# Chunk attention with a cosine router: v loaded by pairs of chunks over all partitions, five tiles ahead

## The chip, the cores and the metric

The kernel runs on one core of one Trainium2 chip. The metric is the device time in microseconds; before the change it is 676.58 us, the median of 3 runs (675.12 to 679.66).

## The reference

Attention works within chunks of 64 positions: batch 8, 8 heads, 576 positions (9 chunks), head size 64, all float32. Its result goes, token by token (4608 tokens of 512), into a mixture of 8 experts with one expert per token.

```python
scores = scale * np.matmul(q_c, k_c.transpose(0, 1, 2, 4, 3))   # per chunk of 64
attn = np.exp(scores - np.max(scores, axis=-1, keepdims=True))
attn = attn / (np.sum(attn, axis=-1, keepdims=True) + 1e-09)
out = np.matmul(attn, v_c)
x = out.transpose(0, 2, 1, 3).reshape(B * S, H * D)
logits = xn @ en.T / tau                     # rows of x and of expert_emb normalised
expert_idx = np.argmax(logits, axis=1)
h = np.maximum(x[mask] @ w1[e], 0.0)         # for each expert e
out[mask] = gate_w[mask, None] * (h @ w2[e])
```

## The kernel before

The order of the work is written out by hand (`manual_schedule`): every engine and every DMA queue takes its instructions in the order in which the code emits them.

**Attention** runs over 36 tiles of 128 tokens, that is two chunks each. Since a batch has 9 chunks, a tile can hold the last chunk of one batch and the first of the next (tiles 4, 13, 22, 31). The 8 heads are 4 pairs; "parity" (`par`) is the head within its pair, even or odd. One pass of the loop at L1037 does, for several tiles at once, the steps of a software pipeline: `turn_qk(t + 3)` (L603) transposes q and k on TensorE; `scores(t + 2)` (L616) multiplies them, in 32 matmuls of 64x64 that use a quarter of the array each, and takes maximum and difference on VectorE; `weights(t + 2)` (L642) is the exponential on ScalarE; `turn_a(t)` (L646) transposes the weights; `values(t)` (L655) multiplies them by v, whose 65th column is 1 so that the row sum comes with it, and divides; `turn_x(t - 1)` (L689) transposes the result. After every four tiles come `logits`, `pick` and `place` (L702, L729, L745), which choose the experts and compute each token's place, and `put` (L810) scatters tile after tile to the DRAM tensor `spots` through GpSimd's queue.

In `scores` the array's rows are chosen by the parity and its columns by the chunk c of the tile. Even heads write one PSUM bank and odd heads another. The transposed weights `aT` therefore have even heads on partitions 0 to 63 and odd heads on 64 to 127, for both chunks, and v has to lie the same way.

**Loads.** `load_qk(t)` (L574) brings q and k of a tile, on GpSimd's queue except the first four k; it runs four tiles ahead of the transposes. `load_v(b)` (L592) brings a whole batch, one DMA a head on SyncE's queue, each onto 64 partitions; two buffers `v_sb` (L457) take turns. The first batch comes in two portions (L1009 and L1048). Batch 1 is issued at the end of step 1 (L1092), and batch b from 2 on (L1064) right after the values of the tile that reads the last chunk of batch b - 2:

```python
b = (2 * t + 2) // NCB + 1
if b not in v_t and b < B and t > 1:
    load_v(b)
```

SyncE's queue also takes, in the order of the code: nine clears of `spots` from step 1 on (L1090), `load_first` of w1 at step NT - 8 = 28 (two DMAs of 2 MB, L1067), the same for w2 at step 30 (L1069), and `load_early` (L807, at steps 26, 27, 28 and 33), which reads the first tokens of experts 0 and 7 back from `spots` and so waits for the puts emitted before it.

**Experts.** Hidden products of the first two blocks (`early_parts`, L1025, from step 34) stand between the last attention tiles. Then come 35 further blocks of 128 tokens in a row, and each reads its w1 and w2 by expert from DRAM.

Of the kernel before, what the change touches and what calls it, by code (L numbers as in the profile page):

```python
# [9 lines left out]
FP32 = mybir.dt.float32  # L10
# [8 lines left out]
P = 128  # L19
CH = 64  # L20
# [5 lines left out]
def kernel(  # L26
# [11 lines left out]
    nc = tc.nc  # L38
    B, H, S, Dh = q.shape
# [3 lines left out]
    NPAIR = H // 2  # L43
    KD = D // P
    KF = F // P
    NT = N // P
    NCB = S // CH
# [39 lines left out]
    def pad(pool, n, name):  # L87

        if n:
            nc.gpsimd.memset(pool.tile([P, n], FP32, tag=name, name=name, bufs=1), 0.0)  # L90
# [33 lines left out]
    def load_first(buf, rows):  # L124

        for s in range(2):
            e = (0, E - 1)[s]
            nc.sync.dma_start(out=whole(buf[s]), in_=rows[:, e : e + 1, :], max_dma_last_dim=4096)
# [316 lines left out]
    VW = 2 * Dh  # L445
    with (
# [7 lines left out]
    ):  # L454

        pad(one, 40, "pad_one")
        v_sb = [one.tile([P, NPAIR, NCB, VW], FP32, name=f"v{i}") for i in range(2)]  # L457
        NX = 2 * RB
        xr = one.tile([P, NX, W], FP32, name="xr")
        blank = one.tile([P, W], FP32, name="blank")  # L460
# [108 lines left out]
            nc.sync.dma_start(out=spots[SPARE : SPARE + G, :], in_=blank[0:G])  # L569

        before = one.tile([P, E], BF16, name="before")
        qk_t, qkT, v_t, st = {}, {}, {}, {}

        def load_qk(t):  # L574

            for src, nm, eng in (
                (k, "kx", nc.sync if t < 4 else nc.gpsimd),
                (q, "qx", nc.gpsimd),
            ):
                x = qk_p.tile([P, H, Dh], FP32, tag=nm, name=nm)  # L580
                done = 0
                while done < P:
                    b, s = divmod(t * P + done, S)
                    n = min(P - done, S - s)
                    eng.dma_start(  # L585
                        out=x[done : done + n],
                        in_=src[b, :, s : s + n, :].rearrange("h p d -> p h d"),
                    )
                    done += n
                qk_t[nm, t] = x.rearrange("p h d -> p (h d)")  # L590

        def load_v(b, c0=0, c1=NCB, eng=nc.sync):  # L592

            t = v_sb[b % 2]
            for h in range(H):
                r0 = CH * (h % 2)
                eng.dma_start(
                    out=t[r0 : r0 + CH, h // 2, c0:c1, 0:Dh],
                    in_=v[b, h].rearrange("(c k) d -> k c d", k=CH)[:, c0:c1],
                )  # L600
            v_t[b] = t

        def turn_qk(t):  # L603
            for nm in ("kx", "qx"):
# [11 lines left out]
        def scores(t):  # L616
            qx, kx = qkT.pop(("qx", t)), qkT.pop(("kx", t))
            ps = ps_s.tile([P, 2, 512], FP32, tag="sc", name="sc")
            sc = ps[:, :, 0 : NPAIR * CH].rearrange("p r (i k) -> p r i k", k=CH)
            for i in range(NPAIR):  # L620
                for par in range(2):
                    for c in range(2):
                        r0, c0 = CH * par, CH * c
                        nc.tensor.matmul(
                            sc[CH * c : CH * c + CH, par, i],
                            lhsT=qx[r0 : r0 + CH, i, c0 : c0 + CH],
                            rhs=kx[r0 : r0 + CH, i, c0 : c0 + CH],
                            start=True,
                            stop=True,
                        )  # L630
            mx = wk.tile([P, 2, NPAIR], FP32, tag="mx", name="mx")
            nc.vector.tensor_reduce(mx, sc, axis=AX.X, op=ALU.max)
            a = wk.tile([P, NPAIR, 2, CH], FP32, tag="a", name="a", bufs=3)
            nc.vector.tensor_tensor(
                a.rearrange("p i r k -> p r i k"),
                sc,
                mx.unsqueeze(3).to_broadcast([P, 2, NPAIR, CH]),
                ALU.subtract,
            )
            st[t] = {"a": a}  # L640

        def weights(t):  # L642
            a = st[t]["a"]
            nc.scalar.activation(a, a, AF.Exp, scale=scale)
# [10 lines left out]
        def values(t):  # L655
            d = st[t]
            ps = ps_v.tile([P, 2, 512], FP32, tag="pv", name="pv")
            pv = ps[:, :, 0 : NPAIR * (Dh + 1)].rearrange("p r (i d) -> p r i d", d=Dh + 1)
            for i in range(NPAIR):
                for par in range(2):  # L660
                    for c in range(2):
                        b, cb = divmod(2 * t + c, NCB)
                        r0 = CH * par
                        nc.tensor.matmul(
                            pv[CH * c : CH * c + CH, par, i],
                            lhsT=d["aT"][r0 : r0 + CH, i, CH * c : CH * c + CH],
                            rhs=v_t[b][r0 : r0 + CH, i, cb, 0 : Dh + 1],
                            start=True,
                            stop=True,
                        )  # L670
            rs = wk.tile([P, 2, NPAIR], FP32, tag="rs", name="rs")
            nc.vector.tensor_scalar(rs, pv[:, :, :, Dh], 1e-9, None, ALU.add)
            nc.vector.reciprocal(rs, rs)
            x = xr[:, t % NX, 0:D]
            nc.vector.tensor_tensor(
                x.rearrange("p (i r d) -> p r i d", r=2, d=Dh),
                pv[:, :, :, 0:Dh],
                rs.unsqueeze(3).to_broadcast([P, 2, NPAIR, Dh]),
                ALU.mult,
            )  # L680
            nc.gpsimd.iota(
                xr[:, t % NX, D + TOK : D + TOK + 1].bitcast(I32),
                pattern=[[0, 1]],
                base=P * t,
                channel_multiplier=1,
            )
            st[t] = {"x": x}
# [106 lines left out]
        def count_early():  # L794

            cnt = rt_ps[:, 3, 0]
            nc.tensor.matmul(cnt, lhsT=onesb, rhs=before, start=True, stop=True)

            nc.vector.tensor_scalar(full, cnt, -1.0, lim, ALU.mult, ALU.add)
            nc.vector.tensor_scalar(full, full, 0.0, float(P), ALU.max, ALU.min)  # L800
            with nc.allow_low_precision("whole numbers up to 36 + 128"):
                nc.vector.tensor_tensor(eqb_all[:, 0], full, ends_e, ALU.mult)
                nc.vector.tensor_tensor(before, before, eqb_all[:, 0], ALU.add)
# [202 lines left out]
        load_qk(1)  # L1006
        for x in v_sb:
            nc.vector.memset(x[:, :, :, Dh : Dh + 1], 1.0)
        load_v(0, 0, 4)  # L1009
        load_qk(2)  # L1010
        load_qk(3)
        norm_experts()
        nc.gpsimd.memset(xr[:, :, D:W], 0.0)
# [23 lines left out]
        for t in range(-3, NT + 3):  # L1037

            if 0 <= t < NT:
                turn_a(t)  # L1040
            if t == early_t - 1:
                count_early()
            if t + 3 < NT:
                turn_qk(t + 3)
                if t + 7 < NT:
                    load_qk(t + 7)
            if t == -2:
                load_v(0, 4, NCB)  # L1048
            if t - 2 in ends:
                logits(ends[t - 2])  # L1050
            if t == NT:
                turn_x(t - 1)
            early_parts(t, 0)
            if 0 <= t + 2 < NT:
                scores(t + 2)
            if t - 2 in ends:
                copy_logits(ends[t - 2])
            if 0 <= t - 1 < NT - 1:
                turn_x(t - 1)
            if t - 3 in ends:  # L1060
                place(ends[t - 3])
            if 0 <= t < NT:
                values(t)
                b = (2 * t + 2) // NCB + 1  # L1064
                if b not in v_t and b < B and t > 1:
                    load_v(b)
            if t == NT - 8:  # L1067
                load_first(w1_sb, w1_rows)
            if t == NT - 6:  # L1069
                load_first([w[0] for w in w2_sb], w2_rows)  # L1070
            if 0 <= t + 2 < NT:
                weights(t + 2)
            if t - 2 in ends:
                pick(ends[t - 2])
            if early_t <= t < early_t + XBUF:
                load_early(t - early_t)

            put(1 if t < NT - 2 else 2)
            if t == NT - 3:
                turn_xb(0)  # L1080
                load_early(XBUF)
            if t == NT - 1:
                turn_xb(1)
            early_parts(t, 1)
            if t == -2:
                turn_experts()
            if t >= 0:
                next(constants, None)
            if t >= 1:
                next(clears, None)  # L1090
                next(clears, None)
            if t == 1:  # L1092
                load_v(1)
        groups()
        pad_places()
        put(len(to_put))
# [23 lines left out]
    with (  # L1120
# [18 lines left out]
        for j in range(LEAST - 1):  # L1139
            n = j + 2  # L1140
# [104 lines left out]
```

## Time and profile before

| | us |
|---|---|
| median of 3 runs | 676.58 |
| profiled execution, its own time | 675.66 |
| its span, first to last instruction | 673.8 |
| first values of tile 0 start | 19.6 |
| values of tile 35 (the last) start | 164.2 |
| second expert product of block 0 starts | 189.5 |
| TensorE matmul busy | 628.7 |
| mean granted TensorE clock | 0.988 of full |

In the profile, PE is TensorE (PEld its weight loads), DVE VectorE, ACT ScalarE, POOL GpSimd; a name with q is the engine's sequencer or DMA queue, so SPq is SyncE's. A row of the timeline has start and length in us, engine, line, operation, output <- inputs, the count, and in brackets the engine's idle time before it and what ended that. A row of the windows has, after the stretch and its length, busy us and instruction count of PE, PEld, DVE, ACT and POOL, then granted clock, DMA share and GB/s. In the page's slices each digit is the busy share in tenths of one fortieth of the span.

### The profile page before, as it was taken

The page shows a single profiled execution, that of the slowest core. Times are in us where ns is not written, and L with a number is a line of the kernel's source. Part 1 is how long each engine was busy: PE and PEld are TensorE (multiplying, and loading weights), DVE is VectorE, ACT ScalarE, POOL GpSimd, SP SyncE. Part 2 cuts the span into 40 slices and gives each one's busy share as a digit, 9 for nine tenths or more (in the row PEclk, how much of TensorE's full clock was granted, in tenths as well). Part 3 has the DMA queues.
Part 4 walks back from the last instruction along what each step waited for, and adds up shares of the span by engine and source line. Part 5 has one row for each costly group of instructions (what it writes and reads, how often), then busy time and mean ns, then how long its engine had stood idle before and what let it go on. Part 6 is the DMA issues. An engine that isn't in the chain of part 4 may idle for free. (4 is left out here: it accounts for less than half of the span.)

```text
span 673.8 us, 24854 instructions
## 1 busy us (share of the span) xinstructions
PE 628.7 (93%) x9744; PEld 366.8 (54%) x9744; DVE 420.9 (62%) x1140; ACT 445.8 (66%) x776; POOL 158.4 (24%) x237
## 2 busy tenths in 40 slices
PE   5989999999789999999999999999999999999993
PEld 4867777776446667667434444334444444444441
DVE  3848888887469555656575466767654666564430
ACT  4746667666124777677877867778777777877650
POOL 6738887743311000000100100001001000100101
PEclk9979999999989999999999999999999999999998
DMA  9998899989918711112777111776821114411101
GB/s 249 235 246 235 240 293 267 266 231 348 363 54 302 279 51 46 43 40 71 293 262 282 57 37 48 281 281 228 330 70 44 44 48 162 172 43 34 51 28 37
DMA packets 94686, 112.66 MB, mean 167 GB/s; under 512 B 52460, under 2 KB 72684, under 8 KB 94552
## 3 DMA queue, kind: packets, MB, share of 16 engines
q1 hardware_dynamic: 82824, 72.84, 33.8%
q0 software_dynamic: 11696, 38.04, 17.1%
q8 instruction: 81, 1.33, 0.8%
q14 instruction: 53, 0.43, 0.2%
q10 hardware_dynamic: 32, 0.02, 0.0%
HBM read 334.71 MB, written 22.69 MB: 530 GB/s over the span
## 5 line engine op out<-in xcount | busy, mean ns | idle before, releaser
L413 PE MATMUL y_ps<-w,hT 128*32 128x512 f32 (+1 forms) x2368 | 272.6, 589 | 0.0
L361 ACT ACTIVATE h<-C 64x256 f32<-64x256 f32 x264 | 178.6, 677 | 95.5 <-DVE C L374 68.9
L413 PEld LDWEIGHTS y_ps<-w,hT 128*32 128x32 f32 x2368 | 103.3, 110 | 142.3 <-issue 110.2
L428 POOL DMA_INDIRECT out_dram<-y,spot x36 | 36.1, 1002 | 436.9 <-ACT y L421 208.8
L374 DVE TENSOR_TENSOR C<-C,h 128x256 f32<-128x256 f32 x231 | 96.1, 416 | 49.2 <-DVEq L299 42.5
L342 PE MATMUL h<-w,S 128*32 128x256 f32 x1056 | 95.6, 379 | 0.0
L342 PE MATMUL h<-sums,xbT 128*32 128x256 f32 x1056 | 94.8, 379 | 0.0
L342 PE MATMUL h<-w,xbT 128*32 128x256 f32 x1056 | 78.5, 380 | 7.1 <-ACTq L299 6.0
L368 DVE STREAM_TRANSPOSE hT<-h 128x512 f32<-128x512 f32 x66 | 46.7, 708 | 44.1 <-ACT h L361 44.0
L342 PEld LDWEIGHTS h<-w,xbT 128*32 128x32 f32 x1056 | 43.0, 110 | 39.8 <-ACTq L299 13.4
L342 PEld LDWEIGHTS h<-w,S 128*32 128x32 f32 x1056 | 50.4, 110 | 20.3 <-ACT w L301 0.4
L342 PEld LDWEIGHTS h<-sums,xbT 128*32 128x32 f32 x1056 | 50.0, 110 | 20.3 <-ACT C L377 0.6
L227 DVE TENSOR_SCALAR rn<-rn 128x1 f32<-128x1 f32 x37 | 5.7, 153 | 68.9 <-ACT rn L224 68.9
L342 PE MATMUL h<-sums,S 128*32 128x256 f32 x528 | 47.8, 379 | 0.0
L813 POOL DMA_INDIRECT spots<-xr,dest x36 | 37.4, 1039 | 30.3 <-DVE dest L778 9.0
L203 DVE STREAM_TRANSPOSE xbT<-xin 128x256 f32<-128x256 f32 x73 | 44.2, 643 | 0.5 <-DVE hT L368 0.5
L224 ACT ACT_TABLE_LOAD x34 | 43.6, 1283 | 0.9 <-issue 0.3
L231 ACT ACT_TABLE_LOAD x34 | 43.6, 1283 | 0.6
L421 ACT ACTIVATE y<-y_ps,gate 128x512 f32<-128x512 f32 (+1 forms) x37 | 25.2, 682 | 24.1 <-issue 8.8
L695 ACT COPY xT<-tr 128x512 f32<-128x512 f32 x36 | 21.1, 586 | 29.8 <-PE tr L693 25.4
L585 POOL DMA_DIRECT2D kx<-in_k_dram x36 | 32.0, 891 | 19.7 <-PE tr L608 18.8
L585 POOL DMA_DIRECT2D qx<-in_q_dram x40 | 34.5, 866 | 1.6 <-PE tr L608 0.8
(202 smaller groups left out, 807.9 us busy)
## 6 DMA issues: line engine op xcount, KB each, us to landing
w<-in_moe_w_dram SPq DMA_DIRECT2D x74, 2048.0 KB
next_w<-in_moe_w_dram SPq DMA_DIRECT2D x67, 2048.0 KB
xin<-spots SPq DMA_DIRECT2D x158, 64.0 KB
qx<-in_q_dram POOLq DMA_DIRECT2D x32, 256.0 KB
v<-in_v_dram SPq DMA_DIRECT2D x56, 144.0 KB
kx<-in_k_dram POOLq DMA_DIRECT2D x28, 256.0 KB
spots<-blank SPq DMA_DIRECT2D x9, 144.0 KB
spot<-spots SPq DMA_DIRECT2D x80, 4.0 KB
```

What stands on the lines that cost most here:

```text
L203: nc.vector.transpose(xT[:, :, cols].rearrange("p c (b i) -> p b c i", i=Q), t[:, s * (D // 2) : (s + 1) * (D // 2)].rearrange("p (b i c) ...
L224: nc.scalar.activation(rn, spot[:, j % SPOTS, SQ : SQ + 1], AF.Sqrt)
L231: nc.scalar.activation(sh, sh, AF.Exp, accum_out=gate)
L342: nc.tensor.matmul(ps[t0 : t0 + Q], lhsT=a[:, c, s], rhs=w[:, r], start=c == 0, stop=c == KD // 2 - 1,)
L361: nc.scalar.activation(h[b][G * v : G * v + G, s].rearrange("p (k i) -> p k i", i=Q), x[G * s : G * s + G].rearrange("p (i k) -> p k i", i=Q),
L368: nc.vector.transpose(hT.rearrange("p k (s b i) -> p b s k i", b=2, i=Q)[:, b], h[b].rearrange("p s (k i) -> p s k i", i=Q),)
L374: nc.vector.tensor_tensor(out, a, b, op)
L413: nc.tensor.matmul(ps[Q * r : Q * r + Q, 0:w], lhsT=d["hT"][:, c, Q * t0 : Q * t0 + Q], rhs=w2_sb[s][buf_of(j)][:, c, d0 : d0 + w], start= ...
L421: nc.scalar.activation(y[:, 0:w], ps[:, 0:w], AF.Copy, scale=gate_of.pop(j))
L428: ins = nc.gpsimd.indirect_dma_start(out=to, out_offset=bass.IndirectOffsetOnAxis(ap=at, axis=0), in_=y[:, 0:w], in_offset=None, bounds_ch ...
L585: eng.dma_start(out=x[done : done + n], in_=src[b, :, s : s + n, :].rearrange("h p d -> p h d"),)
L813: ins = nc.gpsimd.indirect_dma_start(out=spots, out_offset=bass.IndirectOffsetOnAxis(ap=at, axis=0), in_=m, in_offset=None, bounds_check=S ...
```

## The change

v is loaded by pairs of chunks that belong to a tile instead of by batch. A buffer for each parity has 8 slots (`NV`); slot w takes pair w, on all 128 partitions, with four pairs of heads side by side. For even heads pair w is chunks 2w and 2w + 1; for odd heads it is 2w - 1 and 2w, so odd heads are shifted by a chunk. A load is split where its two chunks lie in different batches. Pairs 0 and 1 are loaded at the start, between the first k loads; then each step t issues pair t + 5 at its top, from step -3 to step 31.

The second chunk of a tile now has its odd heads on partitions 0 to 63 and its even heads on 64 to 127, for v and for the weights. So `scores` puts the second chunk's scores in the other parity's bank (`par ^ c`), and `values` takes rows `CH * (par ^ c)`. For an odd head's second chunk, `values(t)` reads slot t + 1.

```diff
-        v_sb = [one.tile([P, NPAIR, NCB, VW], FP32, name=f"v{i}") for i in range(2)]
+        NV = 8
+        v_sb = [one.tile([P, NV, NPAIR, VW], FP32, name=f"v{i}") for i in range(2)]
...
-        def load_v(b, c0=0, c1=NCB, eng=nc.sync):
-
-            t = v_sb[b % 2]
-            for h in range(H):
-                r0 = CH * (h % 2)
-                eng.dma_start(
-                    out=t[r0 : r0 + CH, h // 2, c0:c1, 0:Dh],
-                    in_=v[b, h].rearrange("(c k) d -> k c d", k=CH)[:, c0:c1],
-                )
-            v_t[b] = t
+        def load_v(w):
+
+            for r in range(2):
+                c0, c1 = max(2 * w - r, 0), min(2 * w - r + 2, 2 * NT)
+                while c0 < c1:
+                    b, cb = divmod(c0, NCB)
+                    n = min(c1 - c0, NCB - cb)
+                    p0 = CH * (c0 + r - 2 * w)
+                    nc.sync.dma_start(
+                        out=v_sb[r][p0 : p0 + CH * n, w % NV, :, 0:Dh],
+                        in_=v[b, r::2, CH * cb : CH * (cb + n), :].rearrange("h p d -> p h d"),
+                    )
+                    c0 += n
...
-                            sc[CH * c : CH * c + CH, par, i],
+                            sc[CH * c : CH * c + CH, par ^ c, i],
...
-                        b, cb = divmod(2 * t + c, NCB)
-                        r0 = CH * par
+                        r0 = CH * (par ^ c)
...
-                            rhs=v_t[b][r0 : r0 + CH, i, cb, 0 : Dh + 1],
+                            rhs=v_sb[par][r0 : r0 + CH, (t + par * c) % NV, i, 0 : Dh + 1],
...
-        load_v(0, 0, 4)
+        load_v(0)
         load_qk(2)
+        load_v(1)
         load_qk(3)
...
+            if t + 5 <= NT:
+                load_v(t + 5)
             if t + 3 < NT:
                 turn_qk(t + 3)
                 if t + 7 < NT:
                     load_qk(t + 7)
-            if t == -2:
-                load_v(0, 4, NCB)
...
                 values(t)
-                b = (2 * t + 2) // NCB + 1
-                if b not in v_t and b < B and t > 1:
-                    load_v(b)
...
-            if t == 1:
-                load_v(1)
```

More of the change, by code (lines that the diff above doesn't have):

```diff
@@ L571 @@
         before = one.tile([P, E], BF16, name="before")
-        qk_t, qkT, v_t, st = {}, {}, {}, {}
+        qk_t, qkT, st = {}, {}, {}
         def load_qk(t):
```

## Prediction

> **What bounds the kernel now.** I read the page first (busy shares and slices), then the chain of waits and the waits by releaser, then TensorE's timeline around the slices in which it falls off, then SyncE's own timeline, because the change moves DMAs on that queue.
>
> ```profile
> PE 628.7 (93%) x9744; PEld 366.8 (54%) x9744; DVE 420.9 (62%) x1140; ACT 445.8 (66%) x776; POOL 158.4 (24%) x237
> ...
> PE   5989999999789999999999999999999999999993
> ...
> DMA  9998899989918711112777111776821114411101
> ```
>
> A slice is 16.8 us. The attention stage is slices 1 to 10 (to 165 us). TensorE is full from slice 3 on but for slices 11 and 12, so time lost or won by TensorE before 190 us goes to the end one for one. The chain that ended last lies wholly in the expert steps after 558 us (products and second matmuls), which the change doesn't touch. From 45 us to the end of attention the waits list no wait of TensorE for q, k or v. Two waits for loads lie before that. The first is tile 2's k, queued behind the first half of v:
>
> ```profile
> 13.29 1.09 PE L608 MATMUL tr<-ident,kx 128*128 128x128 f32 x4 [2.27 <-DMA kx<-in_k_dram]
> ```
>
> The second is tile 4, whose second chunk is the first of batch 1; it waits head by head for the burst of eight v loads (the timeline of TensorE, then the windows with clock and DMA share):
>
> ```profile
> 32.94 0.45 PE L664 MATMUL pv<-v,aT 64*64 64x65 f32 x12
> ...
> 35.48 0.33 PE L664 MATMUL pv<-v,aT 64*64 64x65 f32 x4 [0.96 <-DMA v<-in_v_dram]
> 36.66 0.48 PE L664 MATMUL pv<-v,aT 64*64 64x65 f32 x4 [0.85 <-DMA v<-in_v_dram]
> 37.97 0.47 PE L664 MATMUL pv<-v,aT 64*64 64x65 f32 x2 [0.82 <-DMA v<-in_v_dram]
> ```
> ```profile
> 30.00:40.00 10.00, 6.63 (x112) 5.42 (x105) 4.75 (x10) 4.64 (x11) 2.77 (x9) 0.82 1.09 281
> 40.00:50.00 10.00, 10.00 (x212) 8.38 (x214) 6.40 (x19) 5.41 (x14) 5.24 (x10) 0.84 0.83 218
> ```
>
> The clock falls to 0.82 and 0.84 with it. The other end of attention is SyncE's queue, where the weights for the experts start:
>
> ```profile
> 137.62 3.75 SPq L153 DMA_DIRECT2D xin<-spots  x2
> ...
> 149.25 1.20 SPq L128 DMA_DIRECT2D w<-in_moe_w_dram  x2
> 150.54 1.54 SPq L153 DMA_DIRECT2D xin<-spots  x2
> 152.13 11.34 SPq L159 DMA_DIRECT2D spot<-spots  x1
> 163.51 1.17 SPq L153 DMA_DIRECT2D xin<-spots  x2
> 164.72 1.77 SPq L159 DMA_DIRECT2D spot<-spots  x1
> 166.54 1.60 SPq L128 DMA_DIRECT2D w<-in_moe_w_dram  x2
> 168.51 1.52 SPq L153 DMA_DIRECT2D xin<-spots  x2
> 170.08 9.90 SPq L159 DMA_DIRECT2D spot<-spots  x1
> ```
>
> Two 2 MB loads go out at 149.25; the third small load after them takes 11.34 us to issue, and SyncE goes on at 163.5, 14.3 us after the weights. The packet records say the same: no 512-byte packet (the token loads) starts on this queue from 153 to 164 us, while the 4,096-byte weight packets run (150.5 to 166.0; the second pair 167.8 to 182.6, that is 16.1 us after its issue). Today no v load stands behind a weight: batch 7's last goes out by 137.3.
>
> **What the skill says.** "DMA: Bandwidth & Descriptors", section "Queues, rings and completion order": SyncE owns one ring on each DMA engine and each ring is consumed in order; the gap in the 512-byte packets agrees. The same page, "Rules for kernel authors", says that two loads of half the partitions gain nothing over one, since both spread over all engines. The trace agrees that a packet costs the same: median 18 ns for 256 bytes in the first 128-partition k loads and in the 64-partition v bursts. "PSUM — Partial Sum Buffer", section "PSUM bank collisions raise a hardware error": different column tiles may write one bank at once, different row tiles may not. No run here shows the new pairing. "TensorE: Matmul & The Clock Gate", section "What's actually happening": about 3.4 us of idleness halves the clock, about as much work restores it; here transposes of four took 1.06 us instead of 0.60 after the stall.
>
> **The change part by part.** Numbers are times from the span's start; tile t's value matmuls are called values(t).
>
> *Bytes and issues.* Removed: 72 v loads (64 to 144 KB). Added: for each pair of chunks an even-head and an odd-head load of 128 KB, plus splits where a batch begins: 40 + 40 = 80. At SyncE's 0.62 us each, 50 us against 45, hidden: SyncE is idle most of attention. The packets stay 256 bytes, 36,864 of them, so the engines' v time stays.
>
> *Start.* Before k of tile 2 the queue now holds 512 KB of k and 192 KB of v, not 512 + 512. The queue moves about 105 GB/s there (4 to 12 us), so it lands some 3 us sooner: the 2.27 us wait goes. Ends: 0 and 2.3; I take -2.2.
>
> *Tile 4.* Its loads now go out in the first 15 us and nothing that tile 4 needs is in a late burst. By 33 us some 8 MB have landed (250 GB/s); q, k through tile 7 and v through pair 5 are 5.5 MB. From values(4) at 32.94 to values(5) at 44.36 is 11.42 us; the like step with logits from values(8) to values(9) is 59.5 - 55.1 = 4.4. So -7.0. Ends: -4.6 (the wait alone) and -7.0.
>
> *Bursts of later batches.* TensorE doesn't wait for them: 0.
>
> *Scores and values.* The same matmuls; scores change only their bank, values their row half. Each column half still sees one bank per row half, so I take 0; ends 0 and +50 (below). Each values(t) now waits for up to four loads, long landed in midstage; at most 1 us in all, taken as 0.
>
> *The tail, where the cost is.* load_v(t + 5) is issued at the top of step t. values(t) reads pair t + 1 for odd heads, so the lead is four tiles. Pairs 34, 35, 36 are issued in steps 29, 30, 31; w1's 4 MB stand in step 28, w2's in step 30. So pair 34 is behind w1, pair 36 behind w1 and w2. With TensorE's times of before (all earlier gains shift everything alike):
>
> load_early(0) waits for the put of step 25:
>
> ```profile
> 127.64 1.05 POOL L813 DMA_INDIRECT spots<-xr,dest  x1 [0.64 <-DMA kx<-in_k_dram]
> ...
> 132.26 1.05 POOL L813 DMA_INDIRECT spots<-xr,dest  x1 [1.63 <-DVE rs L673]
> ```
>
> It ends at 128.7, lands about 2.5 us later (that much passed between a put and the wait for its slot at 154.5 to 157.4): 131.2. Six token loads 4 us (3.5 for the undisturbed set at 145.74) -> 135.2; pair 32 1.3 -> 136.5; load_early(1) 3.5 -> 140.0; pair 33 1.3 -> 141.3. Then w1, 8 us sooner than today since the batch-7 burst no longer stands ahead. SyncE is held for the 14.3 us seen today -> 155.6; the rest of load_early(2), 3.0 (163.51 to 166.5) -> about 159; pair 34 is issued to 160.4 and lands near 162.2. Pair 35 -> 161.7, w2 from there; pair 36 is issued at 163.3 but lands when w2 has: 161.7 + 16.1 + 1 = about 179.
>
> ```profile
> 157.06 0.70 PE L664 MATMUL pv<-v,aT 64*64 64x65 f32 x32
> ...
> 160.36 0.69 PE L664 MATMUL pv<-v,aT 64*64 64x65 f32 x32
> ...
> 164.18 0.70 PE L664 MATMUL pv<-v,aT 64*64 64x65 f32 x32
> ```
>
> These are values(33), (34), (35). values(33) waits 157.1 to 162.2, +5.1. values(35), then due at 169.3, waits to 179, +9.7. TensorE is in order: the early expert parts, turn_x, logits and the last placement are queued behind it, and DVE, ScalarE and the last puts wait for those. Sum 14.8; ends 11 (chain 4 us sooner) and 19 (load_early(0) as slow as today's 8.1 us). After the second stall the clock is low again: 38.37 to 42.99 took 4.6 us for some 2.8 us of warm work, so +2.0 (0 to 3). The first stall's low clock is inside the second wait.
>
> Sum: -2.2 - 7.0 + 14.8 + 2.0 = +7.6. Profiled execution 675.66 (span 673.8 and 1.9 around it) -> 683.3; it lies 0.9 under the median of 676.58, so in terms of the median 684.
>
> **Rivals.**
> (1) Faster: pairs 34 and 36 arrive in time, because SyncE gets ahead of the weights or the rings serve the small loads beside them. Then only -9.2 stays: 667.4. Against it: the 11.34 us issue and the empty stretch of 512-byte packets. It decides below a tail delay of 2.4 us (9.2 less the 1%, 6.8). Chance 0.15.
> (2) Within 1%: the stalls come, but less shows. From 182.3 to 189.5 TensorE issues 16 expert matmuls in 7.2 us for no cause that the trace names, while 16 took 1.0 just before; if the stall gives it time to recover, up to 6 return: 678. A SyncE chain 4 us sooner does the same: 680. Chance 0.29.
> (3) Much slower: two row halves writing one bank no longer overlap. Then 0.69 us per 32 matmuls becomes 1.38, twice a tile: 2 x 0.69 x 36 = 50, about 730. Against it: no column half meets a bank from two row halves. Chance 0.03.
> (4) The forecast, 684; own range 680 to 691. Chance 0.53.
>
> **How the numbers follow.** Range 675 to 691: it leaves out (1) and (3), 0.18. About 1% is what a measurement of this kernel can tell from no change. Faster is (1): 0.15; within 1% (669.8 to 683.3) is (2): 0.29; slower is (3) and (4): 0.56.
>
> **What would show it.** Right at the start: values(5) under 5 us after values(4), clock 1.00 from 30 to 50 us. Right at the tail: TensorE waits for v at tiles 33 and 35, 4 to 11 us each; the last v packets come after the 4,096-byte packets of w2; expert steps unchanged. Wrong: no wait for v after tile 28, or pv and sc groups longer than 0.75 us.

## The result, and the profile after

The changed kernel takes 685.47 us (median of 5 runs, 682.48 to 686.22) against 675.85 for the kernel before (5 runs, 670.35 to 679.66): ratio 1.0147 on record, 95% interval 1.0113 to 1.0182 (the quotient of the two medians is 1.0142). It is slower, by about 1.5%. The profiled execution took 684.66 with a span of 682.9, against 675.66 and 673.8; the difference of the spans, 9.1 us, is what the two traces have to explain.

The first rows to read are the page's slices, as for the kernel before. A slice is now 17.1 us.

```profile
PE   6899999944798979999999999989999999999993
PEclk9999999986899999999999999999999999999997
DMA  9989999899026821111768211775831114411101
```

The dip of TensorE's row has moved. Slice 3 (34 to 51 us) is full where the kernel before fell to 8, and slices 9 and 10 (137 to 171 us) have become two 4s, with the granted clock low beside them. The windows give the two ends of attention in numbers (stretch and length, busy us and count of PE, PEld, DVE, ACT and POOL, then clock, DMA share, GB/s):

```profile
30.00:40.00 10.00, 8.04 (x194) 6.85 (x193) 6.29 (x14) 6.01 (x15) 4.47 (x10) 1.00 1.01 284
40.00:50.00 10.00, 9.41 (x242) 8.09 (x241) 9.38 (x27) 7.18 (x18) 8.11 (x14) 1.00 0.80 202
...
150.00:160.00 10.00, 4.40 (x75) 3.69 (x75) 3.26 (x12) 1.69 (x4) 0.12 (x1) 0.50 0.82 265
```

From 30 to 50 us the clock is 1.00 where it was 0.82 and 0.84, and TensorE issues 436 matmuls where it issued 324. From 150 to 160 it is 0.50.

**Start of attention**, TensorE's timeline. The loads of k no longer hold tile 2 up, and tile 4 no longer waits head by head:

```profile
10.62 1.11 PE L613 MATMUL tr<-ident,kx 128*128 128x128 f32 x4
...
31.15 0.45 PE L668 MATMUL pv<-v,aT 64*64 64x65 f32 x12
33.00 0.57 PE L668 MATMUL pv<-v,aT 64*64 64x65 f32 x20 [1.40 <-issue]
...
37.29 0.62 PE L668 MATMUL pv<-v,aT 64*64 64x65 f32 x25
```

The row of tile 2's k has no wait in brackets (2.27 us before). From values(4), at 31.15, to values(5), at 37.29, is 6.14 us (11.42 before); a pause of 1.40 us inside values(4) stays, for which the trace names no releaser.

**End of attention**, the same view:

```profile
146.51 0.34 PE L668 MATMUL pv<-v,aT 64*64 64x65 f32 x6
155.33 1.12 PE L668 MATMUL pv<-v,aT 64*64 64x65 f32 x26 [8.48 <-DMA v<-in_v_dram]
156.38 1.11 PE L655 MATMUL tr<-ident,a 128*128 128x128 f32 x4
...
164.02 0.34 PE L668 MATMUL pv<-v,aT 64*64 64x65 f32 x6 [0.24 <-ACT aT L657]
171.79 1.13 PE L668 MATMUL pv<-v,aT 64*64 64x65 f32 x26 [7.43 <-DMA v<-in_v_dram]
```

These are values(33) and values(35). Six of the 32 matmuls of each tile are issued, then the tile stands: the second chunks of odd heads read slot t + 1, that is pair 34 and then pair 36. After the first stall a group of four transposes takes 1.11 us instead of 0.66, and the 32 matmuls of values(34), at 158.90, take 1.15 instead of 0.69.

The queue shows why, in SyncE's own timeline:

```profile
134.42 1.44 SPq L128 DMA_DIRECT2D w<-in_moe_w_dram  x2
135.96 4.64 SPq L153 DMA_DIRECT2D xin<-spots  x2
140.65 5.96 SPq L159 DMA_DIRECT2D spot<-spots  x1
146.65 1.68 SPq L153 DMA_DIRECT2D xin<-spots  x2
148.37 1.72 SPq L159 DMA_DIRECT2D spot<-spots  x1
150.19 3.73 SPq L602 DMA_DIRECT2D v<-in_v_dram  x4
153.96 1.05 SPq L128 DMA_DIRECT2D w<-in_moe_w_dram  x2
155.11 0.66 SPq L602 DMA_DIRECT2D v<-in_v_dram  x1
```

w1 goes out at 134.42; the three token loads behind it hold SyncE until 146.65, 12.2 us; the four loads of pairs 34 and 35 go out only at 150.19, and pair 36 stands behind w2. By the packet records no 256-byte packet of v moves on this queue from 138 to 150 us, those of pairs 34 and 35 run from 151 to about 156, and those of pair 36 from 167 to about 172, at the very end of w2's 4,096-byte packets (155 to 169).

From there the delay reaches the end. Start times in us from the span's start:

| | before | after | after - before |
|---|---|---|---|
| values(0) | 19.6 | 16.3 | -3.3 |
| values(5) | 44.4 | 37.3 | -7.1 |
| values(9) | 59.6 | 53.2 | -6.4 |
| values(33) | 157.1 | 146.5 | -10.6 |
| values(35), its first matmul | 164.2 | 164.0 | -0.2 |
| last placement (first rank product) | 175.9 | 184.7 | +8.8 |
| last pad put (the last of the blank rows that GpSimd puts into `spots`) | 187.5 | 196.3 | +8.8 |
| second product of block 0 | 189.5 | 191.2 | +1.7 |
| second product of block 1 | 205.0 | 205.0 | 0 |
| second product of block 4 | 243.8 | 251.1 | +7.3 |
| second product of the last of the 37 blocks | 659.0 | 667.7 | +8.7 |

Attention had a head start of 10.6 us when it reached tile 33 and lost 19.4 in three tiles and what follows them. The rows of blocks 0 and 1 are the surprise, and experiments 5 and 6 are about them.

### The profile page after: what moved, and what is told of

It reads as the page before. It is cut to its first block, busy times and chain, and to the rows that moved or that the text cites. A ratio compares the mean times of both kernels' runs of the same rounds, so it can differ in the third digit from the quotient of the medians.

```text
span 682.9 us, 24878 instructions
## 1 busy us (share of the span) xinstructions
PE 624.1 (91%) x9744; PEld 350.5 (51%) x9744; DVE 421.4 (62%) x1140; ACT 444.6 (65%) x776; POOL 157.5 (23%) x237
## 5 line engine op out<-in xcount | busy, mean ns | idle before, releaser
L413 PEld LDWEIGHTS y_ps<-w,hT 128*32 128x32 f32 x2368 | 93.4, 110 | 154.4 <-issue 126.0
L342 PE MATMUL h<-w,S 128*32 128x256 f32 x1056 | 98.0, 379 | 1.8 <-DVE w L291 1.8
L342 PE MATMUL h<-sums,xbT 128*32 128x256 f32 x1056 | 96.8, 379 | 0.0
L342 PEld LDWEIGHTS h<-w,xbT 128*32 128x32 f32 x1056 | 41.1, 110 | 42.8 <-ACTq L299 13.4
L668 PE MATMUL pv<-v,aT 64*64 64x65 f32 x1152 | 27.9, 232 | 19.0 <-DMA v<-in_v_dram 15.9
L421 ACT ACTIVATE y<-y_ps,gate 128x512 f32<-128x512 f32 (+1 forms) x37 | 25.2, 682 | 29.1 <-issue 15.9
```

The source lines that it names most:

```text
L342: nc.tensor.matmul(ps[t0 : t0 + Q], lhsT=a[:, c, s], rhs=w[:, r], start=c == 0, stop=c == KD // 2 - 1,)
L413: nc.tensor.matmul(ps[Q * r : Q * r + Q, 0:w], lhsT=d["hT"][:, c, Q * t0 : Q * t0 + Q], rhs=w2_sb[s][buf_of(j)][:, c, d0 : d0 + w], start= ...
L668: nc.tensor.matmul(pv[CH * c : CH * c + CH, par, i], lhsT=d["aT"][r0 : r0 + CH, i, CH * c : CH * c + CH], rhs=v_sb[par][r0 : r0 + CH, (t + ...
```

## The experiments

Theory: the loss is the order of SyncE's queue at the end of attention alone, pairs 34 to 36 behind 2 x 4 MB of weights; with them ahead, the change is faster than the kernel before. Rivals: the new layout costs time everywhere (exchanged banks and rows, more and other DMAs); or TensorE's lost time is only one of several chains, and the end follows another. Times of runs stand against the kernel before on the same chip, whose median was 675.0 to 678.7 in these sets.

**1. Pairs 34 to 36 ahead of w1** (after, changed):

```diff
-            if t + 5 <= NT:
+            if t + 5 <= NT - 3:
                 load_v(t + 5)
...
             if t == NT - 8:
+                for x in range(NT - 2, NT + 1):
+                    load_v(x)
                 load_first(w1_sb, w1_rows)
```

> The changed kernel with pairs 34, 35 and 36 of v issued in step 28 ahead of w1 instead of in steps 29 to 31 behind the weights. Theory (the three pairs queue behind 8 MB of weights on one queue): no wait for v from tile 28 on, values of tile 35 start near 154 us (they are 10.6 us ahead of the kernel before when they reach tile 33), and the gain of the early stage stays whole: 664 to 668 us, ratio to before 0.98 to 0.99. Rival (the two waits come from the DMA engines being full with weights at that time, wherever the pairs stand): w1 goes out only 2 us later, so waits of some us remain, and the time stays above 676.

Measured: 667.93, ratio 0.9893 (0.9865 to 0.992). Both waits for v are gone, and the sign of the change turns over: with these pairs ahead, it gains about 1% (0.8 to 1.35 by the interval). It isn't free: values(35) starts at 156.2, not near 154; w1 goes out 4.9 us later than in the changed kernel, and the first expert product then waits inside tile 34 (TensorE's timeline of this kernel; the releaser named is VectorE, which had finished within tile 34's own values, so a late load is the likelier one):

```profile
149.20 0.69 PE L668 MATMUL pv<-v,aT 64*64 64x65 f32 x32
151.42 3.08 PE L253 MATMUL h_ps<-w,xbT 128*32 128x256 f32 x32 [1.53 <-DVE rs L677]
...
156.23 0.70 PE L668 MATMUL pv<-v,aT 64*64 64x65 f32 x32 [0.22 <-ACT aT L657]
```

**2. Only pair 36 ahead of w2** (after, changed): the cause split in two.

```diff
-            if t + 5 <= NT:
+            if t + 5 < NT:
                 load_v(t + 5)
...
             if t == NT - 6:
+                load_v(NT)
                 load_first([w[0] for w in w2_sb], w2_rows)
```

> The changed kernel with only pair 36 moved, to just ahead of w2 in step 30; pairs 34 and 35 stay behind w1. Theory: the wait at tile 33 stays (8 to 9 us), the wait at tile 35 (7.4 us) goes, and with it the low clock that follows it (about 2 us): 675 to 677 us, level with before. Rival (the waits are not additive, w2 in the rings holds whatever comes): 680 or more.

Measured: 674.07, ratio 0.9987 (0.9972 to 1.0003), a little better than expected, and 1.6% of 675, some 11 us, better than the changed kernel. Its timeline of TensorE keeps the first wait and loses the second:

```profile
154.75 1.13 PE L668 MATMUL pv<-v,aT 64*64 64x65 f32 x26 [9.04 <-DMA v<-in_v_dram]
...
163.44 0.70 PE L668 MATMUL pv<-v,aT 64*64 64x65 f32 x32 [0.24 <-ACT aT L657]
```

The two stalls add; neither hides in the other. Pair 36, one load of 64 KB (256 packets) in the wrong place, is worth 11 us, and with pairs 34 and 35 still late the change comes out even.

**3. Pairs 34 to 36 on ScalarE's queue** (after, changed): same step, another queue.

```diff
-        def load_v(w):
+        def load_v(w, eng=nc.sync):
...
-                    nc.sync.dma_start(
+                    eng.dma_start(
...
-                load_v(t + 5)
+                load_v(t + 5, nc.scalar if t + 5 > NT - 3 else nc.sync)
```

> The changed kernel with pairs 34, 35 and 36 issued at the same steps, but on ScalarE's DMA queue instead of SyncE's. Theory (order within SyncE's rings, and SyncE held at issue): the pairs don't wait for the weights any more, land within 3 to 5 us beside them, and the time is 664 to 669 us. Rival (bandwidth of the shared DMA engines): the waits at tiles 33 and 35 stay above 4 us each, 676 or more.

Measured: 669.61, ratio 0.9911 (0.9877 to 0.9946), a little over the upper end. The waits at tiles 33 and 35 are gone, so the data needn't wait for the weights on another queue. But ScalarE must issue these loads itself, in order with its own work (its timeline):

```profile
126.59 0.57 ACT L657 COPY aT<-tr 128x512 f32<-128x512 f32 x1
128.96 4.73 ACTq L602 DMA_DIRECT2D v<-in_v_dram  x2
133.73 0.58 ACT L616 COPY kxT<-tr 128x512 f32<-128x512 f32 x1 [6.57 <-DMA spot<-spots]
```

ScalarE stands from 127.2 to 133.7; the two issues alone take 4.73 us of it (what the 1.8 us before them wait for, the trace doesn't say), where two by SyncE at 124.26 us in the changed kernel took 1.15. From values(28) to values(29), 124.9 to 135.8, TensorE needs 10.9 us instead of the 4.4 of that step in the changed kernel. Part of the stall was not removed but moved to another step and another engine.

**4. The old layout with batch 1 early** (before, changed): the start's gain without the layout.

```diff
             if t == -2:
                 load_v(0, 4, NCB)
+                load_v(1)
...
-            if t == 1:
-                load_v(1)
```

> The kernel before, with the load of batch 1 of v issued in step -2 behind the rest of batch 0, instead of after step 1; nothing else. Theory (the gain is the timing of batch 1's load, not the layout over all partitions): values of tile 5 start under 5 us after those of tile 4, and 667 to 670 us. Rival (half-partition loads are what is slow): tile 4 still waits several us for v, or the early q and k come late instead, 673 to 677.

Measured: 672.29, ratio 0.9977 (0.9956 to 0.9999). values(4) to values(5) takes 5.1 us (33.07 to 38.13), about as expected, but only 1.5 us (0.23% of 675) reaches the end: 672.29 lies between the ranges of theory and rival. The next tiles give back part: VectorE waits for the landing of earlier puts before it may overwrite their source (its timeline):

```profile
53.72 0.69 DVE L675 TENSOR_TENSOR xr<-pv,rs 128x512 f32<-128x512 f32 x1 [3.11 <-DMA spots<-xr,dest]
...
58.96 0.69 DVE L675 TENSOR_TENSOR xr<-pv,rs 128x512 f32<-128x512 f32 x1 [2.15 <-DMA spots<-xr,dest]
```

So the tile-4 burst is not where all of the changed kernel's 10.6 us comes from.

**5 and 6. Forty idle transposes on TensorE**, once before the last placement and once behind it (after, changed); their output isn't used.

```diff
+        def fill(n):
+            ps = ps_t.tile([P, NPAIR, P], FP32, tag="tr", name="tr")
+            for i in range(n):
+                nc.tensor.transpose(ps[:, i % NPAIR], ident, ident)
...
                 turn_x(t - 1)
+                fill(40)                     # 5
...
         early_parts(NT + 3, 0)
+        fill(40)                             # 6
```

> The changed kernel with 40 more TensorE transposes of the identity into a spare PSUM tile (about 5 us, their result unused), put after the transposes of tile 35 and so ahead of the last logits and the last placement. Theory (the end hangs on the last placement: its puts, then the first gathered token loads and expert weights, 464 us before the last block in every profile so far): the whole 5 us shows, 690 to 691 us. Rival (the end hangs on TensorE's own work): the same 5 us here; the next run tells the two apart.

> The changed kernel with the same 40 transposes put after the last early expert part, when the last placement has been computed. Theory (the end hangs on the last placement and the loads that follow it; TensorE has slack there, it waits 4.5 us for weights at block 4): less than 1 us shows, 685 to 687 us. Rival (as the prediction had it, time that TensorE loses before 190 us goes to the end one for one): 690 to 691 us, as in the run before.

Measured: 688.72, ratio 1.0203 (1.0164 to 1.0242), for the first, and 683.6, ratio 1.0121 (1.0085 to 1.0158), for the second, each some 1.4 us below the range expected for it; the 5.1 us between the two are as expected. The profiled spans are 687.9 and 682.7, against 682.9 without them. TensorE's timelines show the same work in two places; first before the placement (L754), then behind it:

```profile
178.21 4.53 PE L1044 MATMUL tr<-ident 128*128 128x128 f32 x40
...
190.59 0.18 PE L754 MATMUL rt_ps<-eqb_all,sltb 128*128 128x32 bf16 x1 [1.40 <-DVE eqb_all L745]
```
```profile
184.57 0.18 PE L754 MATMUL rt_ps<-eqb_all,sltb 128*128 128x32 bf16 x1 [1.40 <-DVE eqb_all L745]
...
191.20 4.59 PE L1044 MATMUL tr<-ident 128*128 128x128 f32 x40
195.84 7.07 PE L413 MATMUL y_ps<-w,hT 128*32 128x512 f32 x64
```

Work of 4.5 us costs 4 to 5 before the last placement (by the ratios and by the spans) and nothing behind it. In 6, block 0 starts 4.6 us later than in the changed kernel (195.8 against 191.2) and the last block at nearly the same time (667.9 against 667.7). TensorE is busy there but has slack. What is as late as the end is another chain: the last placement (+8.8 us), the puts, the last of them at 196.3 (+8.8), and the token loads that read `spots` back (199.07 after, 190.23 before, +8.8). In the changed kernel TensorE's slack ends at block 4, where it waits for weights:

```profile
251.10 8.60 PE L413 MATMUL y_ps<-w,hT 128*32 128x512 f32 x62 [4.51 <-DMA w<-in_moe_w_dram]
```

In the traces of all the kernels here, from the last pad put to the second product of the last block is 470.1 to 472.5 us, whatever happened before (the 464 us of the expectation count to the block ahead of the last). The rival on the chain holds: what counts is when the last placement is done. Which load carries the delay from the puts to block 4 was not tried.

**7. A lead that grows** from 5 to 8 pairs between steps 17 and 23, with nine slots (after, changed): the pairs creep ahead, so that none is left for the weights' steps and no burst arises.

```diff
-        NV = 8
+        NV = 9
...
+        sent = 2
         for t in range(-3, NT + 3):
...
-            if t + 5 <= NT:
-                load_v(t + 5)
+            while sent <= min(NT, t + 5 + max(0, min(3, (t - 14) // 3))):
+                load_v(sent)
+                sent += 1
```

> The changed kernel with 9 slots instead of 8 and the lead of the v loads growing from 5 tiles to 8 between steps 14 and 23, so that all pairs up to 36 are issued by the top of step 28, ahead of w1 and before the early token loads hold the queue. Theory (the run with the three pairs issued in a lump lost 3 us because w1 went out 4.9 us later and its first product waited): w1 goes out at 132 to 135 us, no wait for v at the end of attention, 663 to 666 us. Rival (the first expert product waits for something other than w1): 667 to 669 as with the lump.

Measured: 664.74, ratio 0.9851 (0.9812 to 0.989); this version beats both kernels. SyncE's timeline at w1, and TensorE's at tiles 33 and 35:

```profile
134.89 0.65 SPq L602 DMA_DIRECT2D v<-in_v_dram  x1
135.58 2.32 SPq L128 DMA_DIRECT2D w<-in_moe_w_dram  x2
```
```profile
144.12 0.70 PE L668 MATMUL pv<-v,aT 64*64 64x65 f32 x32
...
153.64 0.69 PE L668 MATMUL pv<-v,aT 64*64 64x65 f32 x32 [0.24 <-ACT aT L657]
```

Pair 36 is the last v load, just ahead of w1; w1 is only 1.2 us later than in the changed kernel; no wait for v is left. Layout, bytes and loads are those of the changed kernel, apart from the ninth slot, so the order of the last pairs costs it 1.0147 - 0.9851 = 2.96% of 675, 20 us (18.9 by the spans of the two profiles). By run 2, 11 of them are pair 36 behind w2. The other 9 are then pairs 34 and 35 behind w1, by this difference alone; no run moved only these two.

**8. The old batches spread** (4, changed): batches 2 to 7 in groups of 3, 3 and 2 heads over three steps.

```diff
                 if b not in v_t and b < B and t > 1:
-                    load_v(b)
+                    v_t[b] = v_sb[b % 2]
+                    due.extend((b, h) for h in range(H))
+                for b, h in due[:3]:
+                    load_v(b, heads=(h,))
+                del due[:3]
```

> The kernel before with batch 1 of v loaded in step -2, and the loads of batches 2 to 7 spread over three steps (three, three and two heads) instead of all eight in one burst; layout by batch and 64 partitions as before. Theory (the midstage of the changed kernel, values of tile 9 to 32, is 4 to 5 us shorter because its v loads come evenly): that stretch falls from 93 or 94 us to 89 or 90, and the time to 667 to 669 us. Rival (the layout over all partitions is what helps): the stretch stays at 93 or more, 671 to 673 us.

Measured: 671.47, ratio 0.995 (0.9925 to 0.9975): missed. From values(9) to values(32) it takes 97.2 us (94.0 before, 93.3 in run 4, 88.9 after). The last heads of batch 7 now stood behind token loads on SyncE and tile 31 waited for them twice (1.01 and 0.93 us), which brought a low clock. The numbers are those that the rival, the layout, had forecast, but because of these waits the run doesn't tell pace from layout.

**9. The pairs in bursts** (after, changed; nine slots as in 7): four pairs at every fourth step.

```diff
-            if t + 5 <= NT:
-                load_v(t + 5)
+            while sent <= min(NT, t + 8) if t >= 0 and t % 4 == 0 else sent <= min(NT, t + 5) and t < 0:
+                load_v(sent)
+                sent += 1
```

> The changed kernel with its layout by pairs kept, but from step 0 on the pairs go out four at a time at every fourth step (8 to 10 DMAs, 1 MB, about the size of the batch bursts of before), pairs 33 to 36 at the top of step 28 and so ahead of w1; 9 slots. No wait for v at the end of attention in either theory. Theory A, the even pace of the loads made the stretch from values(9) to values(32) shorter (88.8 after, 94.0 before): with bursts it goes back to 92 to 95, the total to 668 to 672. Theory B, the layout by pairs on all partitions did it: the stretch stays at 88 to 90.5, the total at 664 to 667.

Measured: 673.53, ratio 0.9944 (0.991 to 0.9979). From values(9) to values(32) it takes 94.6 us, as long as with the batches and 5.9 longer than in 7, which has the same layout, slots and bytes and differs in when the loads go out. The windows of this stretch, with bounds rounded to 0.1 us, first 7, then 9:

```profile
51.80:140.60 88.80, 82.75 (x2041) 71.16 (x2040) 77.94 (x203) 64.11 (x143) 69.91 (x105) 1.00 0.93 267
52.00:146.70 94.70, 84.28 (x2041) 71.49 (x2040) 78.00 (x203) 65.13 (x143) 71.79 (x107) 1.00 0.90 264
```

Theory A fits and theory B does not: with the layout by pairs, bursts make the middle stretch long. The size is less sure than 5.9. The changed kernel and runs 1, 2, 5 and 6 have the same code in this stretch, and their profiles show 88.9, 90.0, 89.7, 91.6 and 90.1 us; against these, the bursts of 9 cost 3 to 6. Nor is a burst always dear: run 4, with the old batches, takes 54.3 us from values(18) to values(32), the changed kernel 54.0 and the kernel before 56.8. The total, 673.53, lies above the range expected, on a chip where the kernel before took 678.7; by the ratio it would be 671.6 against the 675.4 of run 7's set. Part of the loss is that w1 too goes out late (140.31): the step from values(34) to (35) takes 7.2 us, as in run 1. How a burst slows the tiles was not settled: in the stretch TensorE's idle time is 6.1 us in 7 and 10.4 in 9, spread over many waits of under 1.2 us.

## Why the prediction was right, and where its steps were not

The forecast was 684.0 (675 to 691) and the measurement is 685.47. The mechanism is as forecast: late pairs behind w1 and w2, with waits at tiles 33 and 35. Undone, they return 20 us (run 7). Terms of the sum against what TensorE's timelines show, up to the last placement:

| term | forecast | measured |
|---|---|---|
| start, to values(0) | -2.2 | -3.3 |
| values(0) to values(5) | -7.0 | -3.8 |
| values(5) to values(9) | 0 | +0.7 |
| values(9) to values(33) | 0 | -4.1 |
| wait at tile 33 | +5.1 | +8.5 |
| the rest up to values(35), low clock | 0 | +1.9 |
| wait at tile 35 | +9.7 | +7.4 |
| the rest after it, low clock | +2.0 | +1.5 |
| sum | +7.6 | +8.8 |

The sum is 1.2 us off, but only because its errors cancel: the start and tile 4 gained 2.1 us less than forecast, the stretch from values(5) to values(33) gained 3.4 for which nothing was forecast, and the end of attention cost 2.5 more. That the number fits so closely is luck; that the kernel became slower, and at which waits, is not.

*Start and tile 4: right in kind, 2.1 us too large together.* The two gave -7.1 at values(5) instead of -9.2. Tile 4 fell to 6.14 us, not to the 4.4 taken from tile 8; the 1.40 us pause inside it makes up most. The lower end given for tile 4, -4.6, is nearer to its 5.3. The sign set for it, under 5 us, is missing in this profile, but the step varies: with the same code up to there it took 4.7 and 4.4 us in runs 2 and 3, and 5.8 to 5.9 in 1, 5 and 6.

*Bursts of later batches at nothing: the step that failed.* The forecast took 0 because TensorE waits for no v in midstage. The stretch from values(9) to values(32) got 5.1 us shorter. Run 9 lays 3 to 6 us of such a stretch to the pace of the loads, within the layout by pairs; whether the pace alone would do it with the old layout stays open (run 8). The argument "no wait names this load" was too narrow: bursts lengthened the stretch without any such wait. That they take their share from the other transfers, and so stretch small waits of other names, is a guess.

*Scores and values at nothing: right.* pv and sc groups of 32 stay at 0.69 to 0.70 us, and rival (3), +50 us, is excluded. The Trainium skill, "PSUM — Partial Sum Buffer", section "PSUM bank collisions raise a hardware error", says that column tiles may share a bank at one time and row tiles may not. Taken by the bank, the new pairing doesn't keep to that: both row halves now write each bank, though from different column halves and so into different partitions. The same section puts the collision of two row tiles at one bank and one quadrant of partitions, and there the halves don't meet. Whether matmuls of both row halves were in one bank at the same moment isn't shown.

*The chain to w1: right, slightly early.* The put and the wait for its slot named for the 2.5 us lie 2.9 us apart, a small slip. load_early(0) starts at 120.52; with the 10.6 us of head start that is 131.1 on the old clock, against 131.2 forecast. w1 at 134.42 is 145.0, against 141.3, and SyncE is held 12.2 us, not 14.3. The two errors partly cancel: pairs 34 and 35 go out at 160.8 on that clock, 1.8 later than the forecast's 159. Their four issues take 3.73 us, and values(33) goes on at 165.9, 3.7 later than 162.2.

*The waits: right in place, wrong in split.* Those 3.7 us, less the six matmuls that went ahead (0.34), make the first wait 8.5 instead of 5.1. On the old clock values(35) is then due at 174.6, 5.3 later than forecast (the 3.7 and the low clock), and pair 36 is there at 182.4, 3.4 later; so the second wait is 7.4, not 9.7, and the sum of both 15.9, not 14.8. By the Trainium skill, "TensorE: Matmul & The Clock Gate", section "What's actually happening", some 3.4 us of idleness halve the clock; the 0.50 of the window from 150 to 160 us agrees.

*"Time lost or won by TensorE before 190 us goes to the end one for one": wrong as a rule, right for these stalls.* Run 5 shows it for time before the last placement; run 6 shows that behind it 4.5 us cost nothing. This is also why rival (2) failed. Its reason did come true: the slow stretch of 16 matmuls in 7.2 us is gone in the changed kernel, and block 0 starts only 1.7 us late. But TensorE had made up time on a chain that doesn't set the end; the puts were 8.8 us late, and block 4 hands the difference back.

*Rival (1)* needed pairs 34 and 36 in time. It fails in the changed kernel and is what runs 1 and 7 build: 667.93 and 664.74 against its 667.4.

## What to carry to other kernels

When a load is cut into small pieces that are issued a fixed number of steps ahead, look at what stands in front of the last pieces on their queue: a piece of 64 KB behind 4 MB of weights cost 11 us here. Let the lead grow ahead of the bulk load, so that nothing with a deadline is left behind it and no burst delays the bulk load. Before a stall or a gain is carried to the end, find which chain reaches the end from there; a busy engine need not be on it.

## What the runs showed of the hardware

- Behind two 2 MB loads on one queue the issue itself of a third small load is held: SyncE stood 12.2 us in the changed kernel, and single issues took 5.96 us there and 12.73 in run 1.
- ScalarE stood 6.57 us around two loads on its own queue (run 3); their issues took 4.73 of it.
- The pace at which the same bytes are requested was worth 3 to 6 us in about 90 (run 9, at 94.6 us, against 88.8 to 91.6 in the profiles with evenly issued pairs), without any wait naming these loads.
- The slow stretch of TensorE in the kernel before (16 matmuls in 7.2 us) doesn't appear after the change; nothing here shows its cause.
